# Five rows of wo loaded as 80, 36 and 12 partitions in a streaming attention kernel

## The chip, the cores and the metric

The kernel runs on one core of a Trainium2 chip. The metric is the device time of one execution in microseconds (us); lower is better. TensorE (PE) multiplies matrices, VectorE (DVE), ScalarE (ACT) and GpSimd (POOL) work on elements, and SyncE (SP) issues the loads from HBM into SBUF, which the core's 16 DMA engines carry out.

## The reference: what is computed

One decoding step for 4 sequences of width 512. Attention with 32 heads of 128 reads a cache of 4096 keys and values for each sequence and head, 268 MB of each. Beside it stands a gated feed-forward block on the same `x`, and a scalar gate per sequence mixes the two.

```python
q = (x @ wq).reshape(B, Sq, H, Dh)
p = softmax(einsum("bhqd,bhkd->bhqk", q, k_cache) * Dh ** -0.5)
a = einsum("bhqk,bhkd->bhqd", p, v_cache).reshape(B, Sq, H * Dh) @ wo
b = (gelu(x @ w_gate) * (x @ w_up)) @ w_down
g = sigmoid((x * gate_w).sum(-1, keepdims=True))
return g * a + (1 - g) * b
```

## The kernel before, in words

The work goes in 32 tiles (`NT`), each one sequence and four heads. A tile's keys are one load of 128 partitions by 16384 numbers (8 MB) into one of two buffers `K`; its values are one such load into the single buffer `V`. DVE multiplies keys by the query and sums (L292, L293), ACT takes the exponentials (L308), PE multiplies them with the values (L261). SP issues every large load from one queue, in program order, each behind a wait for its buffer: keys when DVE has let the buffer go (`k_free`), values when PE has finished the tile before.

The last loads are weights, and they reuse the key buffers. `w_gate` and `w_up` go into the first key buffer (`f`); `w_down` and the first 18 rows of `wo` go into the second (`down`), as one load of 10 rows (`W0`) and one of 8. A row here is 512 numbers in each of 128 partitions; a partition's rows lie one behind the other in HBM, so a load of 10 rows takes 20 KB for each partition. When the feed-forward part no longer needs the first buffer (`have_hT`, L375), SP issues the last 14 rows in pieces of 6, 4, 2, 1 and 1 (`PIECES`). Their sizes fall so that PE has little left to do after the last of them.

PE takes the rows in order in `last_sums` (L493): the rows of `w_down`, then 10 rows of `wo` after `ready_o`, then 8, then the pieces. `ready_o` is one mark that POOL sets when DVE has the attention output in place (`have_OX`) and the load of ten has landed (L409). `last_rows` (L524) takes the last four rows, L419 copies the result and SP stores it. A load adds 16 to its semaphore when all of it has landed; the program's `load` (L162) returns that mark.

Of the kernel before, what the change touches and what calls it, by code (L numbers as in the profile page):

```python
# [34 lines left out]
def tile_gated_mix(ctx: ExitStack, tc: tile.TileContext, x, kc, vc, wq, wo, w_gate, w_up, w_down, gate_w, out):  # L35
    nc = tc.nc
    P = 128
    B, H, S, D = kc.shape
    DM = x.shape[2]
# [10 lines left out]
    DR = F // P  # L50
    FG = F // 4
    W1 = (TW - DR * DM) // DM
    WR = TW // DM
    W0 = 10
    PIECES = (6, 4, 2, 1, 1)
    WIDE = 2
    W2 = W1 + sum(PIECES[:WIDE])
    BASE = 24576
# [51 lines left out]
    def semaphore(name):  # L110
        counters.append(ctx.enter_context(nc.semaphore(name)))
        return counters[-1]
# [27 lines left out]
    def both(*marks):  # L140
        PL.wait(*marks)
        return PL.do(nc.gpsimd.nop())  # L142
# [17 lines left out]
    def load(dst, src, sem=None, name=None, engine=nc.sync):  # L160
        sem = sem or semaphore(name)
        engine.dma_start(dst, src).then_inc(sem, 16)  # L162
        return sem, 16
# [22 lines left out]
    p0 = PL.do(nc.gpsimd.memset(ident, 0.0))  # L186
# [88 lines left out]
    f, down = K[0], K[1]  # L275
# [70 lines left out]
    wo_rows = wo.rearrange("(p i) n -> p (i n)", i=WR)  # L346
    SP.wait((k_free, NT - 1))
    for s, a in enumerate((w_gate, w_up)):
# [2 lines left out]
    load_v(L1)  # L351
    SP.wait((k_free, NT))
    got_down = load(down[:, :DR * DM], w_down.rearrange("(p i) n -> p (i n)", i=DR), name="got_down")
    got_wo = [load(down[:, (DR + r0) * DM:(DR + r1) * DM], wo_rows[:, r0 * DM:r1 * DM], name=f"got_wo{r0}")
              for r0, r1 in ((0, W0), (W0, W1))]

    spare = f[:, 2 * KC * F:2 * KC * F + 4 * FG].rearrange("p (a n) -> p a n", n=FG)
    u0, u1, t1, t2 = (spare[:, a, :] for a in range(4))
# [21 lines left out]
    r0 = 0  # L380
    for n in PIECES:
        got_w.append(load(f[:, r0 * DM:(r0 + n) * DM], wo_rows[:, (W1 + r0) * DM:(W1 + r0 + n) * DM],
# [23 lines left out]
    for b in range(B):  # L406
        have_OX = DV.do(nc.vector.tensor_copy(OX[:, :, b], OW[:, b, W2:, None].to_broadcast([P, WR - W2, 8])))

    ready_o = both(have_OX, got_wo[0])  # L409
    AC.wait(pe_mark["wide"])  # L410
    have_a = AC.do(nc.scalar.activation(gs, acc_a, AF.Copy))
    let_go(nc.scalar)
# [15 lines left out]
    def mark(name, instruction):  # L428
        assert PE.do(instruction) == pe_mark[name]
# [52 lines left out]
    def project(count):  # L482
        for _ in range(count):
            n, (kind, r) = next(todo)
            l = hT[:, r, :] if kind == "h" else OW[:, :, r]
            if kind == "h":
                row = down[:, r * DM:(r + 1) * DM]
            elif r < W1:
                row = down[:, (DR + r) * DM:(DR + r + 1) * DM]
            else:  # L490
                row = f[:, (r - W1) * DM:(r - W1 + 1) * DM]
            c = n % 4
            t = nc.tensor.matmul(acc_a[32 * c:32 * c + B], l, row, start=n < 4, stop=n >= len(rows) - 4)  # L493
        return t

    def last_sums():
# [7 lines left out]
        PE.wait(ready_o)  # L504
        project(W0)
        PE.wait(got_wo[1])
        project(W1 - W0)
        for k in range(WIDE):
            PE.wait(got_w[k])
            t = project(PIECES[k])  # L510
        mark("wide", t)

    def last_rows():
        late = [k for k, n in enumerate(PIECES) for _ in range(n)]
        for i in range(W2, WR):
            if i == W2 + 2:
                PE.wait(have_a)
                for c in range(4):
                    nc.tensor.matmul(acc[32 * c:32 * c + 32], pick_b.rearrange("p b k -> p (b k)"),
                                     gs[:, c * P:(c + 1) * P], start=False, stop=False)  # L520
            PE.wait(got_w[late[i - W1]])
            for c in range(4):
                r0 = (i - W1) * DM + c * P
                t = nc.tensor.matmul(acc[32 * c:32 * c + 32], OX[:, i - W2].rearrange("p b k -> p (b k)"),  # L524
                                     f[:, r0:r0 + P], start=i == W2, stop=i == WR - 1)
        mark("all", t)
# [53 lines left out]
```

## Time and profile before

| what | value |
|---|---|
| time, median of 3 runs | 1310.66 us (1310.58 to 1311.02) |
| the profiled execution's own time | 1311.06 us |
| its span in the profile | 1309.3 us |
| busy: DVE, PE, ACT | 88%, 29%, 8% |
| HBM read | 564.67 MB, 431 GB/s over the span |
| DMA engines busy in nearly every fortieth of the span | 90% or more |

The time holds 1.8 us that the span does not. Loads overlap everything else, and the queue of SP runs some 30 to 40 us ahead of what lands. The profile counts a DMA packet where it starts; the packets below 512 B in these rows are the 4-byte increments by which a DMA engine reports its part of a load.

### The profile page before, as it was taken

The numbers are of one execution on the slowest core, as the hardware profiler recorded it, in microseconds if no ns is written. First come the engines' busy times: TensorE is split into PE (matmuls) and PEld (weight loads), VectorE is DVE, ScalarE is ACT, GpSimd is POOL, SyncE is SP. The second block draws the span as 40 slices with busy tenths as digits, with TensorE's granted clock in tenths as the row PEclk, the third lists the DMA queues.
The fourth block names the chain that finished last, engine by engine and source line by source line (L and its number), as shares of the span: only waits on it lengthen the run. The fifth ranks groups of instructions, "written<-read, shape, count | busy, mean of one in ns | idle before, by whom it ended". The sixth has DMA issues, their size and how long they took to land. (4 is left out here: it accounts for less than half of the span.)

```text
span 1309.3 us, 6807 instructions
## 1 busy us (share of the span) xinstructions
PE 385.6 (29%) x2669; PEld 120.8 (9%) x2669; DVE 1146.4 (88%) x270; ACT 109.2 (8%) x363; POOL 0.7 (0%) x6
## 2 busy tenths in 40 slices
PE   3033123333213333311332321233331133332157
PEld 1010001101000110000110100011000011100012
DVE  2999999999999999999999999999999999999950
ACT  1010010000000000000000000000000000000010
POOL 0000000000000000000000000000000000000000
PEclk9565566666556666656666656666655666665578
DMA  9999999999999999999999999999999999999998
GB/s 401 432 447 418 447 418 447 426 440 444 420 447 418 447 418 446 426 438 447 420 447 418 446 418 447 426 438 447 420 447 418 447 418 447 422 442 447 412 438 357
DMA packets 11147, 564.75 MB, mean 431 GB/s; under 512 B 1248, under 2 KB 1280, under 8 KB 1672
## 3 DMA queue, kind: packets, MB, share of 16 engines
q1 hardware_dynamic: 11128, 564.68, 99.7%
q8 instruction: 3, 0.05, 0.0%
q10 hardware_dynamic: 16, 0.02, 0.0%
HBM read 564.67 MB, written 0.02 MB: 431 GB/s over the span
## 5 line engine op out<-in xcount | busy, mean ns | idle before, releaser
L292 DVE TENSOR_TENSOR k<-k,QB 128x16384 f32<-128x16384 f32 (+1 forms) x33 | 551.4, 16708 | 66.5 <-DVEq L151 62.1
L293 DVE TENSOR_REDUCE SC<-k 128x128 f32<-128x16384 f32 x32 | 551.0, 17220 | 4.7
L261 PE MATMUL bank<-v,PM 128*16 128x512 f32 x2048 | 295.1, 741 | 560.0 <-DMA v<-in_A_v_cache 560.0
L261 PEld LDWEIGHTS bank<-v,PM 128*16 128x16 f32 x2048 | 62.2, 114 | 766.2 <-DMA v<-in_A_v_cache 562.8
L256 PE MATMUL bank<-RS,ones 128*128 128x4 f32 x64 | 18.9, 365 | 309.1 <-ACT PM L308 309.1
L321 ACT ACTIVATE o<-bank 128x512 f32<-128x512 f32 x31 | 18.5, 597 | 859.7 <-ACTq L151 859.7
L308 ACT ACTIVATE PM<-SC,nm 32x128 f32<-32x128 f32 x128 | 66.0, 515 | 217.8 <-ACTq L151 216.3
L256 PEld LDWEIGHTS bank<-RS,ones 128*128 128x128 f32 x64 | 16.1, 312 | 315.2 <-ACT PM L308 315.2
L266 PE MATMUL bank<-pick,o 128*128 128x4 f32 x256 | 33.8, 255 | 26.1 <-ACT o L321 25.3
L266 PEld LDWEIGHTS bank<-pick,o 128*128 128x128 f32 x256 | 31.0, 191 | 55.6 <-ACT o L321 53.9
L300 DVE RECIPROCAL ri<-bank 128x4 f32<-128x4 f32 x32 | 5.8, 182 | 22.6 <-DVEq L151 22.6
L308 ACT ACTIVATION_READ_ACCUMULATOR PM<-SC,nm 32x1 f32 x128 | 25.0, 195 | 0.0
L295 DVE TENSOR_REDUCE m<-SC 128x1 f32<-128x128 f32 x32 | 9.1, 286 | 7.6 <-DVEq L151 7.6
L439 PE MATMUL bank<-v,xT 128*32 128x512 f32 x64 | 9.3, 736 | 17.1 <-POOLq L142 13.2
L238 DVE COPY QT<-bank 128x16 f32<-128x16 f32 x8 | 0.9, 179 | 15.2 <-PE bank L447 15.2
L253 ACT ACTIVATE QB<-bank 128x128 f32<-128x128 f32 x32 | 8.9, 277 | 43.0 <-ACTq L151 42.5
L301 DVE TENSOR_TENSOR OT<-bank,ri 128x4 f32 (+1 forms) x32 | 5.2, 161 | 7.5 <-DVEq L151 7.2
L296 DVE STREAM_TRANSPOSE mt<-m 128x32 f32<-128x32 f32 x32 | 6.7, 211 | 4.7
L250 PE MATMUL bank<-ident,QX 128*128 128x128 f32 x33 | 10.2, 309 | 1.4 <-ACT QX L247 1.4
L419 DVE COPY res<-bank 128x128 f32<-128x128 f32 x1 | 0.3, 292 | 11.3 <-PE bank L524 11.3
L297 DVE TENSOR_REDUCE nm<-mt 128x1 f32<-128x32 f32 x32 | 6.0, 186 | 4.8 <-DVEq L151 2.1
L247 ACT ACTIVATE QX<-QT 128x128 f32 (+1 forms) x32 | 9.9, 308 | 2.4 <-DVE QT L238 1.6
(56 smaller groups left out, 58.3 us busy)
## 6 DMA issues: line engine op xcount, KB each, us to landing
v<-in_A_wq SPq DMA_DIRECT2D x2, 4096.0 KB, 16.8
k<-in_A_k_cache SPq DMA_DIRECT2D x2, 4096.0 KB, 35.2
k<-in_B_w_gate SPq DMA_DIRECT2D x1, 3584.0 KB, 31.4
k<-in_B_w_up SPq DMA_DIRECT2D x1, 3584.0 KB, 39.5
k<-in_B_w_down SPq DMA_DIRECT2D x1, 3584.0 KB, 29.0
k<-in_A_wo SPq DMA_DIRECT2D x1, 2560.0 KB, 34.8
k<-in_A_wo SPq DMA_DIRECT2D x1, 2048.0 KB, 39.2
k<-in_A_wo SPq DMA_DIRECT2D x1, 1536.0 KB, 33.6
```

Of the source, the lines that this page charges most:

```text
L247: return nc.scalar.activation(QX, tile_of(QT, pair, s)[:, :, None].to_broadcast([P, HT, PH]), AF.Copy)
L250: return nc.tensor.transpose(qp[:, :D], QX.rearrange("p h k -> p (h k)"), ident)
L253: nc.scalar.activation(QB[s], qp[:, :D], AF.Copy, scale=scale).then_inc(a_to_d, 1)
L256: return nc.tensor.matmul(tot, ones, RS, start=True, stop=True)
L261: return [nc.tensor.matmul(po[32 * (j % 4):32 * (j % 4) + M], p[:, j * M:(j + 1) * M], V[:, j * RJ * D:(j + 1) * RJ * D], start=j < 4, sto ...
L266: return [nc.tensor.matmul(quo, o[:, j * D:(j + 1) * D], pick[:, j, :], start=j == 0, stop=j == RJ - 1) for j in range(RJ)]
L292: then(nc.vector.tensor_tensor(part, part, QB[s][:, None, :].to_broadcast([P, n, D]), op=OP.mult))
L293: then(nc.vector.tensor_reduce(SC[s], k, axis=AX.X, op=OP.add))
L295: then(nc.vector.tensor_reduce(m1, SC[s], axis=AX.X, op=OP.max))
L308: t = nc.scalar.activation(PM[q, :, h], SC[s][q, :], AF.Exp, bias=NM[s][q, :], scale=1.0, accum_out=RS[q, h:h + 1])
L321: nc.scalar.activation(o, po, AF.Copy).then_inc(o_to_p, 1)
L439: t = nc.tensor.matmul(PO[s][32 * j:32 * j + 32], xT[:, c, :], w[:, c, n0:n0 + HB * D], start=c == 0, stop=c == KC - 1)
```

## The change

The load of ten rows becomes four loads. Its first five rows come as three loads by partitions: 0 to 79, 80 to 115 and 116 to 127, all on one semaphore `ahead_o`. Its last five rows come as one load of 128 partitions. POOL waits for all four before it sets `ready_o`. The bytes, the places they go to and all later loads are as they were.

```diff
+    WU = 5
     got_down = load(down[:, :DR * DM], w_down.rearrange("(p i) n -> p (i n)", i=DR), name="got_down")
+    ahead_o = semaphore("ahead_o")
+    for p0, p1 in ((0, 80), (80, 116), (116, P)):
+        load(down[p0:p1, DR * DM:(DR + WU) * DM], wo_rows[p0:p1, :WU * DM], ahead_o)
     got_wo = [load(down[:, (DR + r0) * DM:(DR + r1) * DM], wo_rows[:, r0 * DM:r1 * DM], name=f"got_wo{r0}")
-              for r0, r1 in ((0, W0), (W0, W1))]
+              for r0, r1 in ((WU, W0), (W0, W1))]
...
-    ready_o = both(have_OX, got_wo[0])
+    ready_o = both(have_OX, (ahead_o, 48), got_wo[0])
```

SP's queue at the end of the stream, before the change (`k_76` is the buffer `down`, `k_75` is `f`, and a shape is partitions by numbers in each):

```order
L162 DMA v<-in_A_v_cache 128x16384 [waits pe]
L162 DMA k_76<-in_B_w_down 128x7168 [waits k_free]
L162 DMA k_76<-in_A_wo 128x5120
L162 DMA k_76<-in_A_wo 128x4096
L162 DMA k_75<-in_A_wo 128x3072 [waits dv]
L162 DMA k_75<-in_A_wo 128x2048
L162 DMA k_75<-in_A_wo 128x1024
```

The same place after the change, where lines are one higher:

```order
L163 DMA v<-in_A_v_cache 128x16384 [waits pe]
L163 DMA k_76<-in_B_w_down 128x7168 [waits k_free]
L163 DMA k_76<-in_A_wo 80x2560
L163 DMA k_76<-in_A_wo 36x2560
L163 DMA k_76<-in_A_wo 12x2560
L163 DMA k_76<-in_A_wo 128x2560
L163 DMA k_76<-in_A_wo 128x4096
L163 DMA k_75<-in_A_wo 128x3072 [waits dv]
L163 DMA k_75<-in_A_wo 128x2048
L163 DMA k_75<-in_A_wo 128x1024
```

One load of 5120 numbers has become four of 2560, ahead of the same wait for `dv`, which is `have_hT`.

## Rows read from the trace of the kernel before

**Rows 1.** The chain of waits, its end: start us, us, what.

```profile
1269.07 0.04 issue
1269.11 36.68 DMA k<-in_A_wo
1305.78 0.04 issue
1305.83 0.47 PE bank L524 x8
1306.30 0.02 issue
1306.32 0.29 DVE res L419
```

**Rows 2.** Stretches of the span: their busy times, clock, DMA share, GB/s.

```profile
core 0: us, PE busy (x) PEld busy (x) DVE busy (x) ACT busy (x) POOL busy (x), PEclk, DMA share, GB/s
1201.41:1220.74 19.33, 11.10 (x73) 3.06 (x73) 17.97 (x6) 1.33 (x4) 0.00 (x0) 0.68 1.00 434
...
1305.52:1305.78 0.26, 0.19 (x8) 0.00 (x0) 0.00 (x0) 0.00 (x0) 0.00 (x0) 1.00 0.00 0
```

**Rows 3.** DMA packets that start from 1304.05 to 1304.33 us.

```profile
DMA packets 43, 0.06 MB, mean 220 GB/s; under 512 B 14, under 2 KB 14, under 8 KB 43
```

**Rows 4.** GB/s in 40 slices from 1304.33 to 1304.55 us, and packets.

```profile
GB/s 0 0 0 0 0 0 0 0 0 0 372 0 0 372 0 0 0 0 0 0 0 0 0 0 372 0 0 0 1 0 0 0 0 0 0 0 0 0 0 372
DMA packets 5, 0.01 MB, mean 37 GB/s; under 512 B 1, under 2 KB 1, under 8 KB 5
```

**Rows 5.** DMA packets that start from 1304.55 to 1304.72 us.

```profile
DMA packets 22, 0.01 MB, mean 72 GB/s; under 512 B 4, under 2 KB 20, under 8 KB 22
```

**Rows 6.** DMA packets from 1304.72 to 1305.30 us, and their queue.

```profile
DMA packets 8, 0.01 MB, mean 25 GB/s; under 512 B 1, under 2 KB 1, under 8 KB 8
...
q1 hardware_dynamic: 8, 0.01, 6.4%
```

**Rows 7.** DMA queues from 1304.72 to 1305.52 us.

```profile
q8 instruction: 1, 0.02, 7.5%
q1 hardware_dynamic: 11, 0.02, 6.0%
```

**Rows 8.** DMA queues from 85.2 to 85.3 us.

```profile
q1 hardware_dynamic: 6, 0.39, 910.9%
q8 instruction: 1, 0.02, 60.5%
```

**Rows 9.** The page's DMA queues: ACT's, two loads of four partitions.

```profile
q10 hardware_dynamic: 16, 0.02, 0.0%
```

**Rows 10.** The same queue from 1.85 to 2.03 us.

```profile
q10 hardware_dynamic: 8, 0.01, 12.6%
```

**Rows 11.** The line of the loads: duration ns min/median/max of an issue.

```profile
L162 SPq DMA_DIRECT2D k<-in_A_wo x7: 328/426/435, 1257.5 to 1269.1; - x7
```

**Rows 12.** What SP's queue waited for: us in total, times, longest.

```profile
SPq L162 <- DVE hT L375: 8.8, 1, 8.8
```

**Rows 13.** The page's DMA issues: KB each, us to landing.

```profile
k<-in_A_wo SPq DMA_DIRECT2D x1, 2560.0 KB, 34.8
```

**Rows 14.** The timeline: start us, us, instruction [idle before, and its releaser].

```profile
1257.54 12.00 SPq L162 DMA_DIRECT2D k<-in_A_wo  x7
...
1295.13 0.12 PEld L493 LDWEIGHTS bank<-k,ow 128*4 128x4 f32 x8 [1.04 <-POOLq L142]
...
1303.31 1.05 PE L493 MATMUL bank<-k,ow 128*4 128x512 f32 x8 [0.56 <-DMA k<-in_A_wo]
1304.42 0.60 ACT L411 ACTIVATE gs<-bank 128x512 f32<-128x512 f32 x1 [15.87 <-PE bank L493]
...
1305.83 0.16 PEld L524 LDWEIGHTS bank<-k,o 128*32 128x32 f32 x8 [0.38 <-DMA k<-in_A_wo]
```

## The prediction, made before the changed kernel ran

> **What bounds the kernel now.** I read the chain of waits first. Its last long link is the transfer of the last row of wo, which lands at 1305.78 us; behind it come only eight matmuls, a copy and the store [rows 1]. DVE is the busiest engine, but at this end it waits for PE and PE waits for the load. Next I read the stretches: in a whole tile the DMA engines are busy all the time and move 434 GB/s [rows 2], which over 16 engines is 27.1 GB/s each. So the end moves only with the moment when the last DMA engine has emptied its queue. A packet of 10,240 B, one partition's five rows, takes 10,240 / 27,100 = 0.378 us of one engine.
>
> Then I looked for whether the 16 engines end together. From 1304.05 to 1304.33 us fourteen increments start, the reports of engines on their share of a load [rows 3]. From 1304.33 to 1304.55 there is one more, beside four packets of 2 KB; it is the 1 in the 29th of 40 slices, at 1304.49 [rows 4]. From 1304.72 to 1305.30 there are seven packets of 2 KB and one increment, at 6.4% of 16 engines, which is one engine of 16 [rows 6], and until 1305.52 three packets more [rows 7]; after that none [rows 2]. So fourteen engines are done by 1304.33, a fifteenth by 1304.49, and one goes on to 1305.52: 1.03 us late against the fifteenth. Its last increment reaches PE 0.26 us after that. Only this one engine sets the end.
>
> No view names an engine by number. One thing is excluded. In the stretch from 1304.55 to 1304.72 stand twenty packets under 2 KB [rows 5]: the sixteen of the small store `out<-ones` and four increments, so a store of four rows runs on four engines; the other two packets, of 2 KB, are the late engine's. The store stands behind each engine's loads in the same queue, so these four engines had emptied theirs while the late one had not. The late engine is one of the other twelve. Where its lag comes from no term rests on; a candidate is the 16 KB instruction packet that one engine fetches at 85 us, in the midst of loads [rows 8].
>
> **The change, part by part.** The bytes are the same; what can change is which engine carries them.
>
> *The split.* Two loads of four partitions made 16 packets: eight of data and eight increments [rows 9], so each of the four engines took one partition. I take it from this that a load's partitions go in equal shares to as many engines as divide them, up to 16, beginning with the same engines. Then 80 partitions are five for each of 16 engines, 36 are three for each of twelve, and 12 are one for each of twelve. Twelve engines carry 5 + 3 + 1 = 9 packets of five rows, the last four carry 5; the one load carried 8 for each. The last four are relieved by 3 x 0.378 = 1.13 us, the twelve take on 0.378 us. [...]
>
> *More packets.* A 2 KB packet comes every 0.08 us (seven in 0.58 us with an increment, [rows 6]) where its bytes alone need 0.0756 us, so a packet costs some 0.005 us beside its bytes. The twelve get 9 + 8 = 17 packets where there were 8 and three increments more, some 0.06 us; the last four get 13 and one increment more, some 0.04 us.
>
> *Three more issues on SP.* At 0.43 us each [rows 11] they are 1.3 us. SP then stands 8.8 us for `hT` [rows 12], which hides them; without that cover the pieces would be issued 1.3 us later, and they still have the 36.7 us of rows 1 until the last lands. I take 0. Up to twelve loads are then outstanding where nine were. If SP could not go on with more than nine, the last three pieces would wait for the three loads at the head to land, with nine loads still queued between: 0 as well.
>
> *A longer wait on POOL.* Behind POOL's wait stands only the mark `ready_o`, and PE behind that. The load of ten landed at 1257.54 + 34.8 = 1292.3 us [rows 13, 14], and POOL let PE go at 1295.13 [rows 14], because DVE was last. There are 2.8 us of room: 0.
>
> *The sum.* If the late engine is one of the last four, it ends at 1305.52 - 1.13 + 0.04 = 1304.43 us. The fifteenth ends at 1304.49 + 0.38 + 0.06 = 1304.93 and is now last, 0.59 us before the old end. If that one is relieved too, the next is at 1304.33 + 0.44 = 1304.77 and the gain is 0.75. All pieces land earlier alike, so PE's `wide` and ACT's copy at 1304.42 go along, and PE stands idle 0.38 us before the last row [rows 14], so nothing there takes the gain back. From the profiled execution: 1311.06 - 0.59 = 1310.47 us. The median of the runs lies 0.40 us under that execution, so I put 1310.1 us.
>
> **The rivals.**
>
> *The late engine is one of the eight between.* Then it gets 0.44 us more: 1310.66 + 0.44 = 1311.1 us. By count this is eight of twelve. Against that: the small transfers sit on four engines that are not late, so work seems dealt from one end, and a fetch that is not dealt so is as likely at the other end. No row decides it; I lean to the last four, two to one. [...]
>
> *The loads of part of the partitions crowd the way into SBUF.* This is the slower side. Rows show 27.1 GB/s for an engine while it writes eight partitions that no other engine writes. Suppose the way into eight such partitions carries no more than that, and the lower 64 partitions have half of the ways. Then the first load's 64 lower partitions need 64 x 0.378 / 8 = 3.02 us instead of 5 x 0.378 = 1.89: 1.13 more. The other two loads lie wholly in the upper half. Spread evenly there, 36 partitions need 1.70 us instead of 1.13 and 12 need 0.57 instead of 0.38: 0.76 more, 1.89 with the first. Unevenly, with all eight partitions of one way in the second load and four of one way in the third, they need 3.02 and 1.51: 1.89 and 1.13 more, 4.15 in all. An engine empties its queue in order, so what the twelve lose here they keep. The end moves by -0.59 + 1.89 = +1.30 to -0.59 + 4.15 = +3.56 us: 1312.0 to 1314.2 us. It decides as soon as it costs the twelve more than 0.59. For it speaks that no other load of this size covers fewer than 128 partitions, so nothing in the trace excludes it. Against it: four packets of 2 KB go to partitions 0 to 3 by four engines between 1.85 and 2.03 us and take 12.6% of 16 x 0.18 us with their increments, 0.36 us in all, so some 0.08 us each [rows 10], no longer than a 2 KB packet in the tail [rows 6]; but 2 KB may be too small to show a crowded way. [...]
>
> *The split does not follow equal shares.* If every partition stays with the engine that it has in a load of 128, each carries its 8 packets as before and only the small costs stay: 1310.7 us. Rows 9 can't tell this for larger loads.
>
> **How the numbers follow.** Forecast, late engine relieved: 0.40. Late engine burdened: 0.20. Crowded ways: 0.30. Split as before: 0.08. Something not thought of that gains much: 0.02. A measurement of this kernel tells about 0.2%, 2.6 us, from no change, so the bounds are 1308.0 and 1313.3 us. The relief, the burden and the split as before lie within them, and so does crowding at its even end, to which I give 0.05 of its 0.30; the uneven end, 1314.2, is slower. That gives faster 0.02, same 0.73, slower 0.25. The forecast's own range is 1309.6 to 1310.6 (a gain of 0.75 at its low end, and the 0.44 by which the three runs spread). To hold 8 in 10 the range must reach the burden and most of the crowding: 1309.5 to 1314.5.
>
> **What would show it.** Right: the last landing at some 1305.2 us, the last increments of the engines within 0.5 us of each other, no stretch of a microsecond at a sixteenth of the DMA share. Burdened: the same lone engine, 0.4 us later. Crowded: the DMA share or the rate falls after `w_down` has landed, four engines end some microseconds before the twelve, and all pieces land 1.3 to 3.6 us later. Split as before: the tail as it stands now. The forecast is wrong if the last landing moves by more than a microsecond either way.

## The result, and the profile after

The change made the kernel slower: 1316.20 us median of 6 runs (1314.83 to 1317.61) against 1310.72 us of 6 runs before (1310.58 to 1311.52). The ratio is 1.0041 with a 95% interval of 1.0028 to 1.0054. The forecast was 1310.1 us and the range ended at 1314.5. The six runs fall into two groups, three at 1314.8 to 1315.4 and three at 1317.0 to 1317.6; the profiled execution, 1314.91 us with a span of 1313.1, is of the lower one, so its account explains 3.8 of the 5.5 us by which the medians differ.

The chain of waits of the changed kernel ends as before (start us, us, what). It answers to [rows 1]: the last load lands at 1309.64 instead of 1305.78 us, 3.86 later, and behind it nothing has changed.

```profile
1267.44 42.21 DMA k<-in_A_wo
1309.64 0.04 issue
1309.69 0.47 PE bank L528 x8
```

The stretches of the changed kernel from the end of `w_down` on, with columns as in [rows 2]:

```profile
1285.00:1287.00 2.00, 1.21 (x12) 0.11 (x4) 0.00 (x0) 0.60 (x1) 0.00 (x0) 1.00 0.99 236
1287.00:1289.00 2.00, 1.97 (x20) 1.29 (x24) 0.59 (x4) 0.00 (x0) 0.00 (x0) 1.00 0.94 200
1289.00:1291.00 2.00, 2.00 (x22) 0.40 (x12) 0.66 (x4) 0.00 (x0) 0.00 (x0) 1.00 1.32 154
1291.00:1293.00 2.00, 1.62 (x12) 0.97 (x8) 0.30 (x2) 0.00 (x0) 0.00 (x0) 1.00 0.67 92
1293.00:1295.00 2.00, 0.00 (x0) 0.00 (x0) 0.42 (x4) 0.00 (x0) 0.00 (x0) 0.78 1.07 449
```

The same stretches of the kernel before:

```profile
1285.00:1287.00 2.00, 2.00 (x24) 0.54 (x20) 0.00 (x0) 0.00 (x0) 0.00 (x0) 1.00 1.07 461
1287.00:1289.00 2.00, 1.18 (x12) 0.40 (x4) 0.00 (x0) 0.60 (x1) 0.00 (x0) 1.00 0.83 358
1289.00:1291.00 2.00, 2.00 (x22) 1.00 (x26) 1.01 (x6) 0.00 (x0) 0.00 (x0) 1.00 1.05 451
1291.00:1293.00 2.00, 2.00 (x20) 0.30 (x8) 0.23 (x2) 0.00 (x0) 0.00 (x0) 1.00 0.96 412
```

The last number is GB/s, the one before it the share of DMA engines that are busy. Over the four stretches the engines are as busy as before (0.98 on average in both), and the rate falls from a half of the old one to a fifth. In these 8 us the kernel before moves (461 + 358 + 451 + 412) x 2 us = 3.36 MB and the changed one 1.36 MB. The missing 2.00 MB are 4.6 us at 434 GB/s. At 1293 us the rate is back.

The tail did become even. This is the count of packets that start from 1308.90 to 1309.45 us; it answers to [rows 3 to 7].

```profile
DMA packets 75, 0.11 MB, mean 197 GB/s; under 512 B 17, under 2 KB 33, under 8 KB 74
```

There are seventeen increments, four of them the small store's, so thirteen of the sixteen engines end their last piece within these 0.55 us, and no packet starts from 1309.40 to the landing. The other three have no increment here: they ended earlier. No engine goes on alone as one did for 1.03 us. Four engines were to be relieved; if three of them are the early ones, the fourth, with the old lag, ends among the others. So the trace fits a late engine that is one of the last four.

One reserve was used up. PE now waits 3.8 us for POOL's mark, that is for the first ten rows (columns as in [rows 14]):

```profile
1296.45 6.68 PE L497 MATMUL bank<-k,ow 128*4 128x512 f32 x36 [3.83 <-POOLq L143]
1304.79 1.89 PE L497 MATMUL bank<-k,ow 128*4 128x512 f32 x12 [1.65 <-DMA k<-in_A_wo]
```

PE still stands idle 1.65 us before the piece of six rows, so the chain stays with the loads.

### The profile page after: what moved, and what is told of

Its sections match the earlier page's. It is cut to its first block, busy times and chain, and to the rows that moved or that the text cites. A ratio compares the mean times of both kernels' runs of the same rounds, so it can differ in the third digit from the quotient of the medians.

```text
span 1313.1 us, 6811 instructions
## 1 busy us (share of the span) xinstructions
PE 383.0 (29%) x2669; PEld 119.9 (9%) x2669; DVE 1146.5 (87%) x270; ACT 109.2 (8%) x363; POOL 0.7 (0%) x6
## 2 busy tenths in 40 slices
DMA packets 11315, 564.75 MB, mean 430 GB/s; under 512 B 1288, under 2 KB 1320, under 8 KB 1712
## 5 line engine op out<-in xcount | busy, mean ns | idle before, releaser
L262 PE MATMUL bank<-v,PM 128*16 128x512 f32 x2048 | 292.1, 735 | 562.0 <-DMA v<-in_A_v_cache 562.0
L497 PE MATMUL bank<-k,ow 128*4 128x512 f32 x56 | 9.6, 745 | 6.0 <-POOLq L143 3.8
```

Source lines behind the costliest of these rows:

```text
L262: return [nc.tensor.matmul(po[32 * (j % 4):32 * (j % 4) + M], p[:, j * M:(j + 1) * M], V[:, j * RJ * D:(j + 1) * RJ * D], start=j < 4, sto ...
```

## The experiments

Every kernel was timed in rounds shared with the kernel before, the first four on one chip (where that one has 1310.98 us), the next four on another (1310.92), the last two on a third (1310.84). Each is compared with the kernel before of its own rounds. The edits are against the changed kernel; `...` in brackets stands for the columns `DR * DM:(DR + WU) * DM`, and where a diff takes nothing out, its lines stand in place of the two that the first diff takes out. POOL always waits for 16 from each load on `ahead_o`; only the second diff shows that line.

Three explanations were tried against each other: crowded ways into SBUF, the way HBM is read, and the number of loads and packets.

**As many loads, all of 128 partitions.**

```diff
-    for p0, p1 in ((0, 80), (80, 116), (116, P)):
-        load(down[p0:p1, ...], wo_rows[p0:p1, :WU * DM], ahead_o)
+    for r0, r1 in ((0, 2), (2, 4), (4, WU)):
+        load(down[:, (DR + r0) * DM:(DR + r1) * DM], wo_rows[:, r0 * DM:r1 * DM], ahead_o)
```

> The first five rows come as three loads of 2, 2 and 1 rows over all 128 partitions, so there are as many loads as in the changed kernel and smaller packets (4 KB and 2 KB instead of 10 KB). Theory of crowded ways into SBUF: nothing is crowded, 1310.7 us, at most 0.2 more. Theory of count (the loss comes from more loads, packets or issues): some 1316 us, as the changed kernel. Theory of reads (the loss comes from the pattern in which HBM is read): the engines read the same rows as before, 1310.7 us.

Measured: 1311.15 us (11 runs) against 1310.98, ratio 1.0001 (0.9992 to 1.0010). Its stretches keep their rate:

```profile
1285.00:1287.00 2.00, 1.24 (x12) 0.11 (x4) 0.00 (x0) 0.59 (x1) 0.00 (x0) 1.00 0.98 398
1287.00:1289.00 2.00, 1.94 (x20) 1.28 (x24) 0.55 (x4) 0.01 (x1) 0.00 (x0) 1.00 1.10 454
```

So the number of loads, issues and packets costs 0.2 us by the medians and 1.3 at the end of the interval, not 5.5.

**Two halves, all engines alike.**

```diff
-    for p0, p1 in ((0, 80), (80, 116), (116, P)):
+    for p0, p1 in ((0, 64), (64, P)):
...
-    ready_o = both(have_OX, (ahead_o, 48), got_wo[0])
+    ready_o = both(have_OX, (ahead_o, 32), got_wo[0])
```

> The first five rows come as two loads, of partitions 0 to 63 and 64 to 127. Every engine carries four and four packets, so no engine is relieved or burdened. Crowded ways: each half has eight ways, so each load needs 64 x 0.378 / 8 = 3.02 us where 1.51 would do, both 3.0 us more: 1313.7 us, and somewhat more if a full way holds up others too; packets of 10 KB take some 0.75 us instead of 0.385. Count: two loads more, less than the changed kernel's loss, 1311 to 1313 us, packets of 0.385 us. Reads: the engines read rows at nearly the distances of the 128-partition load, 1310.7 us, packets of 0.385 us.

Measured: 1315.51 us (5 runs), ratio 1.0035 (1.0021 to 1.0048). Its packets from 1285.5 to 1288.5 us:

```profile
DMA packets 79, 0.65 MB, mean 215 GB/s; under 512 B 16, under 2 KB 16, under 8 KB 16
```

79 less 16 increments are 63 packets of 10 KB in 3 us on 16 engines, 0.76 us each where [rows 2] give 0.378. The rate is 215 GB/s, eight times an engine's 27.1. So no uneven share is needed for the loss. The loss, 4.5 us, is 1.5 us larger than the 3.0 of the arithmetic.

**Eight loads of 16 neighbours.**

```diff
+    for p0 in range(0, P, 16):
+        load(down[p0:p0 + 16, ...], wo_rows[p0:p0 + 16, :WU * DM], ahead_o)
```

> The first five rows come as eight loads of 16 neighbouring partitions, one packet for each engine in each. [...] Count: eight loads more, at most 8/3 of the changed kernel's loss of 5.5 us, up to 1325 us, but with packets of 0.385 us and gaps between them. Reads: no number; neighbouring rows lie 64 KB apart, so anything from 1310.7 us up.

Measured: 1317.81 us (5 runs), ratio 1.0052 (1.0038 to 1.0065); a loss of 6.8 us, 2.3 more than the halves'. The rate is 154 GB/s where the halves' was 215:

```profile
1287.00:1289.00 2.00, 1.01 (x10) 0.66 (x13) 1.03 (x6) 0.00 (x0) 0.00 (x0) 1.00 1.04 154
```

The direction fits crowded ways: fewer neighbours in a load, a lower rate. The next load, which goes to other places, may overlap the one before; no run tests this alone.

**The same places, read from a dense block of HBM.** The values of these five rows are not the reference's.

```diff
+    dense = wo[:P * WU].rearrange("(p i) n -> p (i n)", i=WU)
     for p0, p1 in ((0, 80), (80, 116), (116, P)):
-        load(down[p0:p1, ...], wo_rows[p0:p1, :WU * DM], ahead_o)
+        load(down[p0:p1, ...], dense[p0:p1], ahead_o)
```

> The changed kernel with its three loads read from one dense block of wo (10 KB for each partition, one behind the other) instead of rows 64 KB apart; the values in those rows are therefore not the right ones. Crowded ways: the same places are written, so the same time as the changed kernel, 1314.8 to 1317.6 us. Reads: the pattern that cost the time is gone, 1310 to 1311.5 us. Count: as the changed kernel.

Measured: 1315.35 us (5 runs), ratio 1.0039 (1.0026 to 1.0053), in two groups again (1315.0 to 1315.4 and 1317.0 to 1317.3). The rates are nearly those of the changed kernel:

```profile
1289.00:1291.00 2.00, 2.00 (x23) 0.69 (x26) 1.24 (x6) 0.00 (x0) 0.00 (x0) 1.00 1.38 164
1291.00:1293.00 2.00, 2.00 (x19) 0.48 (x10) 0.00 (x0) 0.00 (x0) 0.00 (x0) 1.00 0.67 82
```

Where these rows lie in HBM makes no difference that shows here. With the number of loads excluded above, this leaves the places that are written.

**80 and 48, no engine relieved.**

```diff
-    for p0, p1 in ((0, 80), (80, 116), (116, P)):
+    for p0, p1 in ((0, 80), (80, P)):
```

> The first five rows as two loads, of partitions 0 to 79 and 80 to 127; 48 partitions are three for each of 16 engines, so every engine carries 5 + 3 = 8 packets as before and none is relieved. If the loss comes from crowded ways: 3.0 us for each load where 1.9 and 1.1 would do, and some 1.4 us more as the halves had it over their 3.0, so 1315 to 1315.6 us, and the former late engine ends alone again. If the loss needs loads on twelve engines (the uneven shares): 1310.7 us. The difference to the changed kernel (1316.2 us) is then what the third load and the twelve engines' ninth packet cost, less what the relief gives.

Measured: 1315.60 us (5 runs), ratio 1.0034 (1.0021 to 1.0048), all within 1314.7 to 1316.1. Stretches:

```profile
1287.00:1289.00 2.00, 1.31 (x12) 1.08 (x16) 0.11 (x1) 0.60 (x1) 0.00 (x0) 1.00 1.10 220
1289.00:1291.00 2.00, 2.00 (x24) 0.52 (x18) 1.13 (x6) 0.00 (x0) 0.00 (x0) 1.00 0.96 143
```

Most of the loss (4.7 of 5.5 us) needs no third load and no uneven share.

**Two loads of 64, even and odd partitions.**

```diff
+    for s in range(2):
+        load(down[s::2, ...], wo_rows[s::2, :WU * DM], ahead_o)
```

> The first five rows as two loads of 64 partitions, the even ones and the odd ones, so that each load reaches all parts of SBUF. Crowding by what a load covers: nothing is crowded, 1310.7 us, packets of 0.385 us. [...]

Measured: 1311.03 us (11 runs) against 1310.92, ratio 1.0000 (0.9991 to 1.0009). From 1285.5 to 1287.0 us it has 64 packets of 10 KB in 1.5 us, 0.375 us each:

```profile
DMA packets 80, 0.66 MB, mean 437 GB/s; under 512 B 16, under 2 KB 16, under 8 KB 16
```

It differs from the halves only in which 64 partitions a load takes (and so in which rows of `wo` it reads, which the dense block showed not to matter), and the whole loss is gone. So the loss comes from loads of neighbouring partitions.

**One row instead of five.**

```diff
-    WU = 5
+    WU = 1
```

> The changed kernel with one row instead of five in the three loads, and nine rows in the load of 128 behind them. Crowded ways: the loss goes with the bytes, a fifth of 5.5 us, 1311.5 to 1312 us. A loss for each load or for each change of engines: as the changed kernel, 1314.8 to 1317.6 us.

Measured: 1311.61 us (11 runs) against 1310.92, ratio 1.0005 (0.9996 to 1.0014); 0.7 us, less than the 1.1 of a fifth, and not clear of zero. Where the loss shows is instructive. From 1284.25 to 1284.75 us run the small packets of the three loads, 83 of 2 KB (108 less 25 increments), 0.096 us each on 16 engines, which is nearly the usual pace. The next stretch, already that of the nine rows, has the low rate.

```profile
DMA packets 114, 0.29 MB, mean 582 GB/s; under 512 B 25, under 2 KB 25, under 8 KB 108
1284.25:1284.75 0.50, 0.50 (x12) 0.14 (x8) 0.00 (x0) 0.00 (x0) 0.00 (x0) 1.00 1.84 582
1284.75:1285.75 1.00, 1.00 (x16) 0.29 (x12) 0.00 (x0) 0.00 (x0) 0.00 (x0) 1.00 0.79 201
```

Packets count where they start, so six large ones that start in the first stretch add to its 582 GB/s. The two stretches together move 0.49 MB in 1.5 us, 328 GB/s.

**120 and 8, by equal shares the sixteenth engine without any of these rows.**

```diff
-    for p0, p1 in ((0, 80), (80, 116), (116, P)):
+    for p0, p1 in ((0, 120), (120, P)):
```

> The first five rows as two loads of partitions 0 to 119 (eight for each of 15 engines) and 120 to 127 (one for each of eight engines). The sixteenth engine carries nothing of these rows, the first eight carry nine packets. [...] Crowding by what a load covers: only the second load is crowded, 1311.5 to 1312.5 us. Which engine was late: if it is the sixteenth, one engine ends some 3 us before the others, and no lone engine ends a microsecond after the rest; if it is another, the lone late one stays.

Measured: 1316.49 us (5 runs), ratio 1.0041 (1.0027 to 1.0055). A load of 120 neighbours, nearly all of the 128 partitions, is slow too:

```profile
1285.00:1287.00 2.00, 2.00 (x20) 0.32 (x12) 0.00 (x0) 0.00 (x0) 0.00 (x0) 1.00 0.96 179
1287.00:1289.00 2.00, 1.18 (x16) 1.04 (x16) 0.00 (x0) 0.60 (x1) 0.00 (x0) 1.00 0.98 215
```

So what a load covers as a whole does not explain every loss. Either what counts is the places that the engines write at the same moment, or a load on 15 engines, as equal shares have it, loses by itself. No kernel here has a load at full rate that goes to fewer than 16 engines by equal shares, so this stays open. One engine goes on alone in the tail, here the queues from 1311.00 to 1311.55 us:

```profile
q8 instruction: 1, 0.02, 16.2%
q1 hardware_dynamic: 7, 0.01, 5.8%
```

If the sixteenth carries none of the 120, as by equal shares, the late engine of this execution is not the sixteenth.

**Uneven shares by strided partitions.** An attempt at a version that beats both.

```diff
-    for p0, p1 in ((0, 80), (80, 116), (116, P)):
-        load(down[p0:p1, ...], wo_rows[p0:p1, :WU * DM], ahead_o)
+    for part in (slice(0, P, 2), slice(1, P, 4), slice(3, 96, 4), slice(99, P, 4)):
+        load(down[part, ...], wo_rows[part, :WU * DM], ahead_o)
```

> The uneven shares of the changed kernel without neighbouring partitions: the first five rows as four loads, of the 64 even partitions, of the 32 that are 1 more than a multiple of 4, and of the 32 that are 3 more, these as 24 and 8. By equal shares the first two give every engine 4 and 2 packets, 24 gives twelve engines two each, 8 gives the first eight engines one each: nine packets for eight engines, eight for four, six for the last four, where one load gave eight. If crowding by neighbours is the whole loss and the late engine is one of the last four: packets of 0.385 us all through, the late engine 0.76 us earlier, eight others 0.38 us later, so the last end moves from 1.03 us behind the fifteenth to about level: 1310.2 to 1310.4 us (0.5 to 0.7 less than the kernel before), and no lone engine for a microsecond in the tail. If the late engine is one of the first eight: 0.4 us more, 1311.3 us, lone engine in the tail. If uneven shares cost time by themselves: 1312 us or more.

Measured: 1311.46 us (11 runs) against 1310.84, ratio 1.0006 (0.9997 to 1.0015), six runs at 1311.0 to 1311.5 and five at 1312.0 to 1312.8. It is no gain. The loads of 64 and 32 run at nearly full rate; with the loads of 24 and 8, by equal shares on twelve and eight engines, the rate falls:

```profile
1285.00:1286.70 1.70, 1.70 (x20) 0.43 (x16) 0.00 (x0) 0.00 (x0) 0.00 (x0) 1.00 0.95 404
1286.70:1289.50 2.80, 1.99 (x20) 1.08 (x16) 0.12 (x1) 0.60 (x1) 0.00 (x0) 1.00 1.02 296
```

Its tail is nearly even all the same. From 1305.25 us to the end of the loads there are thirteen increments, four of them the store's, so nine engines end their last piece within 0.7 us:

```profile
DMA packets 47, 0.06 MB, mean 85 GB/s; under 512 B 13, under 2 KB 29, under 8 KB 46
```

**The same with 32 in one load.**

```diff
+    for part in (slice(0, P, 2), slice(1, P, 4), slice(3, P, 4)):
+        load(down[part, ...], wo_rows[part, :WU * DM], ahead_o)
```

> As the run before it, with the last 32 partitions in one load: every engine carries eight packets again, so there is no relief and no crowding. Both theories: as the kernel before, 1310.7 to 1311.1 us, and one engine ends a microsecond after the others; the difference to the run with 24 and 8 is the relief alone, 0.5 to 0.7 us.

Measured: 1310.79 us (11 runs) against 1310.84, ratio 1.0000 (0.9991 to 1.0009).

```profile
1286.70:1289.50 2.80, 2.28 (x22) 1.30 (x26) 0.90 (x5) 0.46 (x1) 0.00 (x0) 1.00 1.01 428
```

Against this control the stretch with the loads of 24 and 8 loses (428 - 296) x 2.8 us = 0.37 MB, 0.85 us at 434 GB/s, more than the relief was to give (0.5 to 0.7). Whether that comes from fewer engines or from the places they write, the two kernels do not tell. None of the variants beats the kernel before.

## Why the prediction was wrong, point by point

- *The bound* was read rightly: the end moves with the last landing, 3.86 us in the profiled execution, and the span with it (3.8).
- *One late engine, relieved* fits the changed kernel's trace. It was a guess that came true: no row before carried the two to one.
- *The split by equal shares* fits: the trace of the changed kernel has 1288 packets under 512 B where the one before has 1248. The 40 increments more are sixteen for the 80 partitions and twelve each for 36 and 12. Thirteen engines end together and three are early, as they would if both loads of twelve begin with the same engines; no view shows that by itself.
- *More packets, three more issues*: the run with as many loads over 128 partitions shows no cost within 1.3 us. SP did come to a stop, which the prediction had allowed for: its last issue took 9.65 us where none took more than 0.44 before [rows 11], and the 42.21 us of the chain contain it. The kernel with 64, 32 and 32 partitions has the same stop and loses nothing, so the 0 was right. Both kernels, in the order named (ns min/median/max):

```profile
L163 SPq DMA_DIRECT2D k<-in_A_wo x10: 313/432/9651, 1257.6 to 1267.4; - x10
L163 SPq DMA_DIRECT2D k<-in_A_wo x10: 328/432/9655, 1257.2 to 1267.0; - x10
```

- *The wait on POOL*: the loads used up the 2.8 us of room and more. PE's wait grew to 3.8 us and is still off the chain.
- *The step that failed* is the sum's price of a packet. It took 0.378 us for each packet of the partial loads, from a row in which every load has 128 partitions. In the changed kernel 38 such packets start from 1285.5 to 1287.0 us, 1.5 x 16 / 38 = 0.63 us each, and from 1289.90 to 1290.60 us start 14 (24 less 10 increments) that take 2.223 x 16 x 0.70 / 14 = some 1.8 us each. The first line is the first of these stretches:

```profile
DMA packets 39, 0.39 MB, mean 259 GB/s; under 512 B 1, under 2 KB 1, under 8 KB 1
DMA packets 24, 0.14 MB, mean 205 GB/s; under 512 B 10, under 2 KB 10, under 8 KB 10
q1 hardware_dynamic: 24, 0.14, 222.3%
```

The rival of crowded ways laid it to the partitions written and had the side and the place, but a chance of 0.30 and 1.3 to 3.56 us. The two runs with 64 partitions show that it is the choice of partitions: halves cost 4.5 us, even and odd cost nothing.

- *The rival's size* was short too. The relief came in full in the profile: the engines that were not late end at 1309.4 instead of 1304.49, 4.9 us later, of which 0.44 are their extra packet and the small costs. So the slow loads cost some 4.5 us, and -0.59 + 4.5 = 3.9 is what the last landing moved. The rival had 1.89 to 4.15 for crowding, because I let each load pay only for itself. That a way takes eight partitions, and the lower 64 half of the ways, was supposed. No run shows which partitions share a way, and so none shows the 4.15 of the uneven end; the runs show 215 GB/s for loads of 64 neighbours and a loss of 4.7 us with 80 and 48. The slow pace spreads: of the 14 packets of some 1.8 us above, the third load has twelve at most, and the load of 128 partitions starts slowly behind them, 92 GB/s from 1291 us.
- *The upper group of runs*, 2 us higher, is not explained by this profile. The dense block shows the same two groups, the strided kernel two that lie some 1.3 us apart. But by equal shares the kernel with one row also has loads on twelve engines, and that with 120 and 8 one on eight, and neither shows a clear gap. What sets the groups stays open, and with it 1.6 of the 5.5 us between the medians.
- *The evidence that misled* was [rows 10]: small packets to four neighbours at their usual pace. The run with one row shows such packets at nearly that pace too, 2 KB each, and the rate falling to 201 GB/s right behind them. So a packet's own time need not show the loss; I had named the doubt and still let the row lower the rival's chance.

That the gain would have come without the slow loads was not shown: no kernel here gives twelve engines more than the others at full rate. The strided kernel, 0.7 us slower than its control, leaves it open: its tail is nearly even, but the low rate of its last two loads costs more than the relief could give.

## What to carry to other kernels

Price a load of part of the partitions by which partitions it takes, not by its bytes alone: here loads of 64 neighbours ran at 215 GB/s and loads of 64 alternate ones at the full 437. Why 120 neighbours are slow as well is not settled here, so a shape that no run has shown is measured first. Relief of a late engine is worth less than its lag, here 0.59 of 1.03 us by the prediction's sum; compare that with what the loads that bring it may cost. When the trace before holds no load of the new shape, small packets that seem to run freely say little of it: here those of 2 KB took 0.096 us each, and the rate fell to 201 GB/s behind them.

## What the runs showed of the hardware

- Behind the loads of 80, 36 and 12 neighbouring partitions the next load was slow too: 92 GB/s in the packets that start from 1291 to 1293 us, most of them of a load of 128 partitions, and 449 GB/s after that.
- The 2 KB packets of three such loads ran at nearly their usual pace (0.096 us each, 0.08 in the tail before [rows 6]), and the rate fell behind them (201 GB/s; 328 over both stretches).
- SP's issue of the last of the ten loads of `wo` took 9.65 us where the median of the ten is 0.43, while earlier loads were still on their way.
- Even and odd partitions in loads of 64 and, with every fourth, of 32 ran at full rate (437 and 428 GB/s); the load of 120 neighbours ran at 179 to 215 GB/s.
- PE's granted clock fell from 1.00 to 0.78 of full speed in the stretch from 1293 to 1295 us, in which PE did nothing.
